# Top-k attention with two MLPs: scores of a head by full-array products, key halves stacked on 128 partitions, and the halves of two weights made by other engines

## The chip, the cores and the metric
One core of one Trainium2 chip runs the whole program in one launch. The metric is the device time of an execution in microseconds; the profile shows one execution of it. PE is TensorE (PEld its weight loads), DVE VectorE, ACT ScalarE, POOL GpSimd, SP the engine that issues the DMAs.

## The reference
Inputs are q, k, v of 4 batches, 8 heads, 576 tokens, 64 elements a head, and five float64 weights. Attention keeps only the 32 largest scores of a row:

```python
scores = scale * np.matmul(q, k.transpose(0, 1, 3, 2))
kth = np.partition(scores, -top_k, axis=-1)[..., -top_k:-top_k + 1]
scores = np.where(scores >= kth, scores, -1000000000.0)
attn = softmax(scores)            # over 576 keys
x = (attn @ v)                    # to 2304 tokens x 512
h = x @ w_in                      # 512 -> 2048
g = np.where(h > 0.0, h, np.exp(np.minimum(h, 0.0)) - 1.0)
x = g @ w_out                     # 2048 -> 512
out = ((x @ w1) * (x @ w2)) @ w3 @ w_out2   # 512 -> 1024 -> 1024 -> 512
```

The choice of the 32 depends on small differences of scores, so the kernel works with high and low halves of its numbers throughout.

## The kernel before
The 2304 tokens are 18 tiles of 128, taken two by two as nine chunks. For each chunk `attention` goes over four head pairs and two tiles, 72 tile-pairs in all; `mlp` then runs the dense layers of the chunk. A tile that spans two batches is scored against both, so there are 80 scored segments for 72 tile-pairs.

Order: each operation is registered with `op(engine, cost, function, reads, writes, rank)`. `Program.emit` then simulates the engines with the written costs, the table `LAT` of handover times, and ranks to which the table `OFF` adds an offset by stage and engine. It writes out one fixed order per engine. An engine's instructions run in that order, so one that waits holds up all behind it on its engine. SP's queue holds all DMAs, loads and transposes alike.

Scores. Queries of a pair and chunk (two heads of 64 rows on 128 partitions, 256 tokens) are loaded into the single buffer `qr`; ACT rounds them to `qh` (L407), POOL makes the rest `ql` (L408). Keys of a batch and pair are loaded once, rounded by ACT (L356) and their rest made by POOL (L357), both into `KT` of 128 partitions by 2 halves by 576, written to DRAM as `KD` and reloaded from there later. For each half of the 576 keys, `qk` (L437) issues six products of 288 columns on half arrays of 64 rows: high with high, high with low, low with high, for two heads each. ACT's L439 then moves the two heads' 288 columns out of `psS`, with the scale. `psS` is one buffer of two banks, so the second half waits for this copy; the columns behind the 288 hold the results of the value product (L491).

Top-k. Per head DVE runs four MAX8 (L447), each but the last followed by a MATCH_REPLACE8 (L449). ACT makes mask and exponential in place (L462, L464), ACT and POOL the two f16 halves (L472, L473), two DMA transposes turn them round, and L491 multiplies by the values.

Weights. Each float64 weight is loaded as words, joined by ACT, DVE and POOL (L542 to L545), normed and converted by `convert`: the high half is a scaled f16 copy; the low half, in the mode used for w_in and w_out, is made on PE as the f32 product with a scaled identity less the high half (L581, L582), and copied out of PSUM (L584). `PAR["hp"]` names the number of sixteenths whose high half POOL makes (L567): all 16 of w_in and all 16 of w_out. w3 and w4 are multiplied with each other first (L686). w1 and w2 are converted with DVE instead (L572).

Dense layers. `unitA` (L747 to L749), `unitO` (L784 to L786) and `unitB` (L826 to L828) issue f16 products of 256 columns, `unitD` (L861 to L863) of 512. Between them ACT, DVE and POOL work on PSUM results; L797 and L846 on DVE are of these, L809 is a small f32 product for a norm.

Of the kernel before, what the change touches and what calls it, by code (L numbers as in the profile page):

```python
# [33 lines left out]
PAR = dict(hp={'wi': 16, 'wo': 16}, whole=(), cd={'wi': [0, 0], 'wo': [0, 0], 'w34': [8, 0], 'w12': [16, 0]}, pv=-577.81, pi=702.591, p34=-453.754, po=123.714, p12=822.408,   # L34
# [5 lines left out]
OFF = {":DVE": 10640, "A0:ACT": 7132, "A0:PE": 7142, "A0:POOL": 10197, "A1:ACT": -310, "A1:PE": -245, "A1:POOL": 1267, "A2:ACT": 133, "A2:PE": -970,  # L40
# [25 lines left out]
       "attsa:ACT": -31679, "attsa:PE": -6029, "attsk:ACT": -21025, "attsk:POOL": 3784, "attsk:SP": 10401, "attsm:ACT": 45222, "attsm:POOL": 39295,  # L66
       "attsp:ACT": -3530, "attsp:POOL": 10399, "attsp:SP": 10858, "attsq:ACT": -8447, "attsq:POOL": 20171, "attsq:SP": 1342, "attss:ACT": 2111,
       "attss:PE": 5478, "attst:DVE": 30531, "attsv:ACT": 22427, "attsv:DVE": 28403, "attsv:SP": 23421, "attsx:ACT": 3955, "attsx:DVE": -7451,
# [3 lines left out]
       "w_in.n:DVE": -17269, "w_in.n:PE": 5551, "w_in:ACT": -10309, "w_in:DVE": -20971, "w_in:POOL": -20121, "w_in:SP": -39372, "w_out.c:ACT": -4070,  # L72
       "w_out.c:PE": -19360, "w_out.c:POOL": -8192, "w_out.n:DVE": -32159, "w_out.n:PE": -3273, "w_out:ACT": -8581, "w_out:DVE": 7470, "w_out:POOL":
       12309, "w_out:SP": -12693, "w_v0:DVE": -38737, "w_v0:PE": 13902, "w_v0:SP": -24224, "w_v1:DVE": -16351, "w_v1:PE": 28175, "w_v1:SP": 59626,
       "w_v:DVE": -23895}
# [120 lines left out]
def kernel(ctx: ExitStack, tc: tile.TileContext, qd, kd, vd, vn, w_in, w_out, w1, w2, w3t, w4, out,  # L196
# [11 lines left out]
    def ring(name, n, shape, dt, space=pool):  # L208
        return [space.tile(shape, dt, name=f"{name}{i}") for i in range(n)]
# [20 lines left out]
    qr = pool.tile([128, 256], F32, name="qr")  # L230
    QH = ring("qh", NQ, [128, 256], F32R)
    QL = ring("ql", NQ, [128, 256], F32R)
# [114 lines left out]
    def att_loads(b, p, pr):  # L347
        ks = nxt("k", NK)
        if ("k", b, p) in seen:
            dma(KT[ks].rearrange("p a s -> p (a s)").bitcast(I32), KD[b, p].bitcast(I32), 128 * S * 8, [("kd", b, p)], [("k", ks)], pr)  # L350
            return ks
        seen.add(("k", b, p))
        rs = nxt("raw", 2)
        kr = raw[rs][:, 0:S]
        dma(kr, kd[b, p], 128 * S * 4, [], [("raw", rs)], pr)
        op("ACT", 574, lambda: A.activation(KT[ks][:, 0], kr, AF.Copy), [("raw", rs)], [("k", ks)], pr)  # L356
        op("POOL", 1240, lambda: G.tensor_tensor(KT[ks][:, 1], kr, KT[ks][:, 0].bitcast(F32), op=OP.subtract),  # L357
           [("raw", rs)], [("k", ks)], pr)
        dma(KD[b, p], KT[ks].rearrange("p a s -> p (a s)").bitcast(F32), 128 * S * 8, [("k", ks)], [("kd", b, p)], pr + PAR["ost"] * STEP)
        return ks  # L360
# [32 lines left out]
    def attention(c, t0, n):  # L393
# [6 lines left out]
        for pair in range(4):  # L400
            base = (t0 * 8 + pair * n * 2 + PAR["a0"] * (c == 0) + PAR["a1"] * (c == 1)) * STEP
            qs = nxt("q", NQ)
            N = n * 128
            pq = base + PAR["oq"] * STEP
            part("q")
            dma(qr[:, 0:N], qd[pair, :, t0 * 128:t0 * 128 + N], 128 * N * 4, [], ["qr"], pq)
            op("ACT", 93 + N * .833, lambda qs=qs: A.activation(QH[qs][:, 0:N], qr[:, 0:N], AF.Copy), ["qr"], [("qh", qs)], pq)  # L407
            op("POOL", 143 + N * 1.904, lambda qs=qs: G.tensor_tensor(QL[qs][:, 0:N], qr[:, 0:N], QH[qs][:, 0:N].bitcast(F32), op=OP.subtract),  # L408
               ["qr", ("qh", qs)], [("ql", qs)], pq)
            for t in range(n):  # L410
                gt = t0 + t
# [578 lines left out]
```

## Time and profile before

| what | value |
|---|---|
| median of 3 runs | 1095.58 us (1093.68 to 1097.67) |
| profiled execution, span of it | 1092.33 us, 1090.5 us |
| busy PE / DVE / ACT / POOL | 998.8 / 870.4 / 806.7 / 694.7 us |
| L437 score products | 960, in groups of six |
| L567 high halves on POOL | 32 |
| L447 MAX8 | 576 |
| first and last first-layer product (L747) | 221.5 and 1023.0 us |

Busy time is the union of an engine's instructions. Matmuls overlap in the pipeline: one of 256 columns is shown with 0.27 us, while the next can start much earlier. So the cost of a group of matmuls is read from starts, not from durations.

### The profile page before, as it was taken

What the parts mean: (1) busy time and instruction counts of PE and PEld (TensorE: products, weight loads), DVE (VectorE), ACT (ScalarE), POOL (GpSimd) and SP (SyncE); (2) the same over time, 40 slices, a digit from 0 to 9 for tenths busy, and PEclk for the clock granted to TensorE, in tenths of its full rate; (3) what the DMA queues carried; (4) which work ended last, traced back from release to release, by engine and by line L of the source; (5) the groups of instructions that cost most, each with busy time, mean ns of one, the idle gap of its engine ahead of it and who ended that gap; (6) DMA issues with size and microseconds to landing.
All of it is one profiled execution on the core that took longest, in us unless ns stands there. A gap on an engine that the chain in (4) does not pass through costs nothing.

```text
span 1090.5 us, 24990 instructions
## 1 busy us (share of the span) xinstructions
PE 998.8 (92%) x9452; PEld 757.9 (69%) x9452; DVE 870.4 (80%) x1936; ACT 806.7 (74%) x1469; POOL 694.7 (64%) x723
## 2 busy tenths in 40 slices
PE   3576789988899999999999999999999999999998
PEld 2323334467788768887886887688768877887875
DVE  4977679999699999989998998978999999742010
ACT  5877587689889967886886778699678868735612
POOL 3999975569838826684784677468447846635711
PEclk9987889999999999999999999999999999999999
DMA  9958799586934766456699436557763563034001
GB/s 317 390 176 237 192 223 268 109 226 203 224 95 143 183 164 155 105 139 134 167 223 240 115 83 169 138 155 190 172 146 87 113 131 69 4 60 88 2 1 39
DMA packets 238681, 165.57 MB, mean 152 GB/s; under 512 B 195808, under 2 KB 208608, under 8 KB 238560
## 3 DMA queue, kind: packets, MB, share of 16 engines
q1 hardware_dynamic: 238560, 163.97, 58.2%
q8 instruction: 74, 1.21, 0.5%
q14 instruction: 47, 0.39, 0.1%
HBM read 95.13 MB, written 21.61 MB: 107 GB/s over the span
## 4 chain that ended last, share of the span: by engine, by line
PE 42%; DVE 17%; DMA 13%; ACT 10%; POOL 10%; issue 6%; SPq 1%; POOLq 0%; DVEq 0%; ACTq 0%
DMA pt<-pi 7%; DVE m L447 7%; DVE wk L449 6%; PE psS L437 4%; PE psR L747 3%; PE psR L749 3%; PE psR L748 3%; PE psY L784 3%; PE psR L826 3%; PE psS L491 3%; PE psY L786 3%; PE psY L785 3%; PE psR L828 3%; PE psR L827 3%; POOL pi L473 2%
## 5 line engine op out<-in xcount | busy, mean ns | idle before, releaser
L447 DVE MAX8 m<-wk 128x8 f32<-128x576 f32 x432 | 310.1, 748 | 0.0
L473 POOL TENSOR_TENSOR pi<-s,pi 128x576 f16<-128x576 f32 x144 | 183.9, 1284 | 105.8 <-ACT pi L472 76.6
L449 DVE MATCH_REPLACE8 wk<-m,wk 128x576 f32<-128x576 f32 x288 | 212.3, 743 | 0.0
L747 PE MATMUL psR<-x,win 128*128 128x256 f16 x576 | 157.2, 273 | 3.1 <-ACT t L768 2.7
L785 PE MATMUL psY<-g,wout 128*128 128x256 f16 x576 | 157.4, 273 | 1.7 <-POOL g L771 1.7
L784 PE MATMUL psY<-g,wout 128*128 128x256 f16 x576 | 157.8, 274 | 0.0
L786 PE MATMUL psY<-g,wout 128*128 128x256 f16 x576 | 157.4, 273 | 0.0
L826 PE MATMUL psR<-x,w 128*128 128x256 f16 x576 | 157.3, 273 | 0.0
L828 PE MATMUL psR<-x,w 128*128 128x256 f16 x576 | 157.0, 273 | 0.0
L749 PE MATMUL psR<-x,win 128*128 128x256 f16 x576 | 157.0, 273 | 0.0
L827 PE MATMUL psR<-x,w 128*128 128x256 f16 x576 | 157.0, 273 | 0.0
L748 PE MATMUL psR<-x,win 128*128 128x256 f16 x576 | 157.0, 273 | 0.0
L439 ACT ACTIVATE s<-psS 128x576 f32<-128x576 f32 (+1 forms) x160 | 103.2, 645 | 60.1 <-POOL pi L473 35.7
L437 PE MATMUL psS<-kt,qh 64*128 64x288 f32 x640 | 90.6, 361 | 32.2 <-ACT s L439 17.7
L447 DVE MAX8 m<-s 128x8 f32<-128x576 f32 x144 | 102.7, 747 | 20.5 <-ACT s L439 20.5
L462 ACT ACTIVATE s<-s,m 128x576 f32<-128x576 f32 x144 | 107.2, 771 | 13.2 <-DVE m L447 12.9
L464 ACT ACTIVATE s<-s,ty 128x576 f32<-128x576 f32 x144 | 106.0, 768 | 6.6 <-POOL ty L458 6.5
L472 ACT ACTIVATE pi<-s 128x576 f16<-128x576 f32 x144 | 95.4, 677 | 19.7 <-DMA pt<-pi 19.5
L437 PEld LDWEIGHTS psS<-kt,qh 64*128 64x128 f32 x640 | 50.9, 196 | 80.3 <-ACT s L439 27.6
L449 DVE MATCH_REPLACE8 wk<-m,s 128x576 f32<-128x576 f32 x144 | 106.2, 744 | 0.0
L769 POOL TENSOR_TENSOR t<-t,t 128x512 f32<-128x512 f32 x72 | 92.2, 1284 | 5.0 <-ACT t L768 3.5
L771 POOL TENSOR_TENSOR g<-t,g 128x512 f16<-128x512 f32 x72 | 83.7, 1164 | 16.1 <-ACT g L770 15.9
(154 smaller groups left out, 2268.6 us busy)
## 6 DMA issues: line engine op xcount, KB each, us to landing
kt<-kd SPq DMA_DIRECT2D x32, 576.0 KB, 4.4
vv<-vd SPq DMA_DIRECT2D x32, 455.0 KB, 4.1
kd<-kt SPq DMA_DIRECT2D x16, 576.0 KB, 4.0
w<-w_in SPq DMA_DIRECT2D x16, 512.0 KB, 6.1
w<-w_out SPq DMA_DIRECT2D x16, 512.0 KB, 8.0
w<-w3t SPq DMA_DIRECT2D x16, 512.0 KB, 5.5
vd<-vv SPq DMA_DIRECT2D x16, 455.0 KB, 4.6
w<-w SPq DMA_DIRECT2D x12, 512.0 KB, 5.0
```

The costliest lines, as they stand in the source:

```text
L447: op("DVE", 665, lambda r=r, src=src, m8=m8, hh=hh: V.max(m8[:, hh, 8 * r:8 * r + 8], src), [skey], [mk], p1 + PAR["ot"] * STEP)
L449: op("DVE", 727, lambda r=r, src=src, w=w, m8=m8, hh=hh: V.match_replace(w, m8[:, hh, 8 * r:8 * r + 8], src, -3.0e38), [skey, mk], [k], p1 ...
L473: op("POOL", 1240, lambda Y=Y, PIs=PIs, hh=hh: G.tensor_tensor(PIs[:, hh, S:2 * S], Y[:, hh], PIs[:, hh, 0:S], op=OP.subtract), hks, [pk], ...
L747: T.matmul(o, lhsT=hi(W)[:, cs], rhs=X[:, 0, kd_, 0:N], start=kd_ == 0, stop=False)
L748: T.matmul(o, lhsT=hi(W)[:, cs], rhs=X[:, 1, kd_, 0:N], start=False, stop=False)
L749: T.matmul(o, lhsT=lo(W)[:, cs], rhs=X[:, 0, kd_, 0:N], start=False, stop=kd_ == 3)
L784: T.matmul(o, lhsT=hi(W)[:, cs], rhs=rh, start=ft == 0 and m % 2 == 0, stop=False, skip_group_check=True)
L785: T.matmul(o, lhsT=hi(W)[:, cs], rhs=rl, start=False, stop=False, skip_group_check=True)
L786: T.matmul(o, lhsT=lo(W)[:, cs], rhs=rh, start=False, stop=ft == 15, skip_group_check=True)
L826: T.matmul(o, lhsT=hi(W)[:, cs], rhs=X[:, 0, kd_, 0:N], start=kd_ == 0, stop=False)
L827: T.matmul(o, lhsT=hi(W)[:, cs], rhs=X[:, 1, kd_, 0:N], start=False, stop=False)
L828: T.matmul(o, lhsT=lo(W)[:, cs], rhs=X[:, 0, kd_, 0:N], start=False, stop=kd_ == 3)
```

## The change
Queries are loaded per tile and pair as two heads side by side, each head's 64 rows twice, on partitions 0 to 63 and 64 to 127. Keys are prepared per head: the 64 rows are loaded twice, ACT rounds all 128 partitions, and POOL replaces partitions 64 to 127 by the rest, so high keys lie over low keys. One product over 128 partitions then holds the high and the low keys for one operand of queries; high and low queries make two products a half of the keys, four a head. The group and its copy out of `psS` are now of one head and all keys. Keys of scores in the dependency table are per head, so a head's top-k depends on its own copy only. The offsets `OFF` and some written costs are other numbers. High halves of w_in and w_out are made by ACT, their low halves leave PSUM by DVE.

```diff
-PAR = dict(hp={'wi': 16, 'wo': 16}, whole=(), ...
+PAR = dict(hv={}, lv={'wi': 16, 'wo': 16}, whole=(), ...
...
-    qr = pool.tile([128, 256], F32, name="qr")
-    QH = ring("qh", NQ, [128, 256], F32R)
-    QL = ring("ql", NQ, [128, 256], F32R)
+    qr = pool.tile([128, 2, 128], F32, name="qr")
+    QH = ring("qh", NQ, [128, 2, 128], F32R)
+    QL = ring("ql", NQ, [128, 2, 128], F32R)
...
-        rs = nxt("raw", 2)
-        kr = raw[rs][:, 0:S]
-        dma(kr, kd[b, p], 128 * S * 4, [], [("raw", rs)], pr)
-        op("ACT", 574, lambda: A.activation(KT[ks][:, 0], kr, AF.Copy), [("raw", rs)], [("k", ks)], pr)
-        op("POOL", 1240, lambda: G.tensor_tensor(KT[ks][:, 1], kr, KT[ks][:, 0].bitcast(F32), op=OP.subtract),
-           [("raw", rs)], [("k", ks)], pr)
+        for hh in range(2):
+            rs = nxt("raw", 2)
+            kr = raw[rs][:, 0:S]
+            dma(kr, kd[b, 2 * p + hh], 128 * S * 4, [], [("raw", rs)], pr)
+            op("ACT", 574, lambda kr=kr, hh=hh: A.activation(KT[ks][:, hh], kr, AF.Copy), [("raw", rs)], [("k", ks)], pr)
+            op("POOL", 1370, lambda kr=kr, hh=hh: G.tensor_tensor(KT[ks][64:128, hh], kr[64:128], KT[ks][64:128, hh].bitcast(F32), op=OP.subtract),
+               [("raw", rs)], [("k", ks)], pr)
...
         for pair in range(4):
-            qs = nxt("q", NQ)
-            N = n * 128
-            pq = base + PAR["oq"] * STEP
-            part("q")
-            dma(qr[:, 0:N], qd[pair, :, t0 * 128:t0 * 128 + N], 128 * N * 4, [], ["qr"], pq)
-            op("ACT", 93 + N * .833, lambda qs=qs: A.activation(QH[qs][:, 0:N], qr[:, 0:N], AF.Copy), ["qr"], [("qh", qs)], pq)
-            op("POOL", 143 + N * 1.904, lambda qs=qs: G.tensor_tensor(QL[qs][:, 0:N], qr[:, 0:N], QH[qs][:, 0:N].bitcast(F32), op=OP.subtract),
-               ["qr", ("qh", qs)], [("ql", qs)], pq)
             for t in range(n):
+                qs = nxt("q", NQ)
+                pq = pr + PAR["oq"] * STEP
+                part("q")
+                dma(qr, qd[2 * pair:2 * pair + 2, :, tok:tok + 128].rearrange("h r t -> r h t"), 128 * 256 * 4, [], ["qr"], pq)
+                op("ACT", 306, lambda qs=qs: A.activation(QH[qs], qr, AF.Copy), ["qr"], [("qh", qs)], pq)
+                op("POOL", 690, lambda qs=qs: G.tensor_tensor(QL[qs], qr, QH[qs].bitcast(F32), op=OP.subtract),
+                   ["qr", ("qh", qs)], [("ql", qs)], pq)
...
-                for half in range(2):
-                    cols = slice(half * 288, half * 288 + 288)
-                    pqk = pr + (PAR["os"] + .25 * half) * STEP
+                for hh in range(2):
+                    pqk = pr + (PAR["os"] + .5 * hh) * STEP
                     for kk, c0, c1 in ks:
-                        def qk(qs=qs, kk=kk, t=t, cols=cols):
-                            for i, (L, e) in enumerate(((QH, 0), (QH, 1), (QL, 0))):
-                                for hh in range(2):
-                                    hs = slice(64 * hh, 64 * hh + 64)
-                                    T.matmul(psS[:, hh, 0:288], lhsT=L[qs][hs, t * 128:t * 128 + 128], rhs=KT[kk][hs, e, cols], start=i == 0, stop=i == 2)
-                        op("PE", 560, qk, [("qh", qs), ("ql", qs), ("k", kk)], ["psS"], pqk)
-                        op("ACT", 540, lambda sS=sS, cols=cols, c0=c0, c1=c1: A.activation(sS[c0:c1, :, cols], psS[c0:c1, :, 0:288], AF.Copy, scale=0.125), ["psS"], [sk], pqk)
+                        def qk(qs=qs, kk=kk, hh=hh):
+                            for half in range(2):
+                                for li, L in enumerate((QH, QL)):
+                                    T.matmul(psS[:, half, 0:288], lhsT=L[qs][:, hh], rhs=KT[kk][:, hh, half * 288:half * 288 + 288], start=li == 0, stop=li == 1)
+                        op("PE", 540, qk, [("qh", qs), ("ql", qs), ("k", kk)], ["psS"], pqk)
+                        op("ACT", 540, lambda ...: A.activation(sS[c0:c1, hh].rearrange("p (a b) -> p a b", a=2), psS[c0:c1, :, 0:288], AF.Copy, scale=0.125), ["psS"], [(*sk, hh)], pqk)
...
-        if spread(i, PAR["hp"].get(nm, 0)):
-            op("POOL", 660, lambda: G.tensor_scalar(hi(W[i]), st, s, None, op0=OP.mult), [*skeys, sk], [(nm, i)], pr)
+        if spread(i, PAR["hv"].get(nm, 0)):
+            op("DVE", 340, lambda: V.tensor_scalar(hi(W[i]), st, s, None, op0=OP.mult), [*skeys, sk], [(nm, i)], pr, lk=True)
         else:
-            op("ACT", 620, lambda: A.activation(hi(W[i]), st, AF.Copy, scale=s), [*skeys, sk], [(nm, i)], pr)
+            op("ACT", 613, lambda: A.activation(hi(W[i]), st, AF.Copy, scale=s), [*skeys, sk], [(nm, i)], pr)
...
-        op("ACT", 480, lambda: A.activation(lo(W[i]), ps, AF.Copy), [pk], [(nm, i, "l")], pr)
+        if spread(i, PAR["lv"].get(nm, 0)):
+            op("DVE", 600, lambda: V.tensor_copy(lo(W[i]), ps), [pk], [(nm, i, "l")], pr)
+        else:
+            op("ACT", 480, lambda: A.activation(lo(W[i]), ps, AF.Copy), [pk], [(nm, i, "l")], pr)
```

## Rows read from the trace of the kernel before

**Rows 1.** The page's busy time, with share of the span and instructions
```profile
PE 998.8 (92%) x9452; PEld 757.9 (69%) x9452; DVE 870.4 (80%) x1936; ACT 806.7 (74%) x1469; POOL 694.7 (64%) x723
```

**Rows 2.** Busy us (instructions) by stage; last three columns PEclk, DMA share, GB/s
```profile
core 0: us, PE busy (x) PEld busy (x) DVE busy (x) ACT busy (x) POOL busy (x), PEclk, DMA share, GB/s
47.00:147.00 100.00, 66.96 (x300) 31.74 (x301) 71.65 (x159) 70.91 (x130) 98.54 (x78) 0.81 0.70 211
147.00:221.00 74.00, 69.63 (x348) 32.58 (x347) 68.97 (x146) 57.73 (x105) 41.51 (x43) 1.00 0.88 207
221.00:327.00 106.00, 93.32 (x1060) 78.46 (x1059) 93.35 (x211) 90.64 (x167) 75.01 (x73) 0.98 0.71 188
327.00:981.00 654.00, 642.11 (x6723) 519.84 (x6722) 593.32 (x1331) 511.57 (x939) 409.05 (x453) 1.00 0.56 137
```

**Rows 3.** Timeline of PE at 884 us: start us, us, instruction
```profile
884.42 0.27 PE L828 MATMUL psR<-x,w 128*128 128x256 f16 x1
...
884.75 0.27 PE L828 MATMUL psR<-x,w 128*128 128x256 f16 x1
884.86 0.39 PE L809 MATMUL psY<-ident,ac 128*128 128x128 f32 x2
885.08 0.27 PE L826 MATMUL psR<-x,w 128*128 128x256 f16 x1
```

**Rows 4.** Timeline of DVE, 943 to 964 us; in brackets idle time before
```profile
943.33 1.42 DVE L447 MAX8 m<-s 128x8 f32<-128x576 f32 x2 [4.32 <-ACT s L439]
...
951.66 1.42 DVE L447 MAX8 m<-wk 128x8 f32<-128x576 f32 x2
962.96 1.41 DVE L797 SCALAR_TENSOR_TENSOR x<-psY,sc,x 128x512 f16<-128x512 f32 x2 [9.89 <-ACT x L796]
```

**Rows 5.** L567 alone by stage: us, POOL busy (instructions), PEclk, DMA share, GB/s
```profile
47.00:147.00 100.00, 50.83 (x32) 0.81 0.70 211
```

**Rows 6.** Timeline of PE around a score group at 502 us
```profile
502.23 0.27 PE L828 MATMUL psR<-x,w 128*128 128x256 f16 x1
502.44 0.54 PE L437 MATMUL psS<-kt,qh 64*128 64x288 f32 x4
502.81 0.29 PE L437 MATMUL psS<-kt,ql 64*128 64x288 f32 x2
503.04 0.39 PE L861 MATMUL psR<-w,pp 128*128 128x512 f16 x1
```

**Rows 7.** The same group, a timeline that ends after its first pair
```profile
502.44 0.40 PE L437 MATMUL psS<-kt,qh 64*128 64x288 f32 x2
```

**Rows 8.** L437 alone by stage: us, PE busy (x), PEld busy (x)
```profile
147.00:981.00 834.00, 96.56 (x870) 62.71 (x870) 1.00 0.61 149
```

**Rows 9.** Groups of instructions: out<-in, count, busy us, mean ns, idle before
```profile
L408 POOL TENSOR_TENSOR ql<-qr,qh 128x256 fp32r<-128x256 f32 x36 | 27.3, 758 | 42.9 <-ACT qh L407 42.2 <-POOL wout L545 0.3 <-ACT ty L502 0.3
L357 POOL TENSOR_TENSOR kt<-raw,kt 128x576 fp32r<-128x576 f32 x16 | 22.6, 1415 | 5.3 <-ACT kt L356 5.3
L407 ACT ACTIVATE qh<-qr 128x256 fp32r<-128x256 f32 x36 | 14.8, 412 | 8.4 <-PE psS L437 5.7 <-DMA qr<-qd 2.6
L569 ACT ACTIVATE w<-w,sc 128x512 f16<-128x512 f32 x21 | 14.5, 713 | 2.1 <-DVE w L572 1.6 <-DVE sc L312 0.4
L797 DVE SCALAR_TENSOR_TENSOR x<-psY,sc,x 128x512 f16<-128x512 f32 x18 | 12.8, 743 | 55.6 <-ACT x L796 55.5
L356 ACT ACTIVATE kt<-raw 128x576 fp32r<-128x576 f32 x16 | 10.9, 681 | 4.1 <-DMA raw<-kd 4.0
L584 ACT ACTIVATE win<-psY 128x512 f16<-128x512 f32 x16 | 9.6, 610 | 2.5 <-PE psY L582 2.5
```

**Rows 10.** L447 alone by stage: us, DVE busy (instructions)
```profile
0.00:221.00 221.00, 70.82 (x100) 0.92 0.82 238
```

**Rows 11.** PE's waits, the longest: us in total, times, longest
```profile
PE psS L437 <- ACT s L439: 17.7, 14, 4.3
```

**Rows 12.** Timeline of PE where the weight product ends and the first layer starts
```profile
220.65 1.02 PE L686 MATMUL psY<-w,pp 128*128 128x512 f32 x2
221.51 0.27 PE L747 MATMUL psR<-x,win 128*128 128x256 f16 x1
```

More of the change, by code (lines that the diff above doesn't have):

```diff
@@ L32 @@
 FLAT = 2.0 ** -100
-PAR = dict(hp={'wi': 16, 'wo': 16}, whole=(), cd={'wi': [0, 0], 'wo': [0, 0], 'w34': [8, 0], 'w12': [16, 0]}, pv=-577.81, pi=702.591, p34=-453.754, po=123.714, p12=822.408,
+PAR = dict(hv={}, lv={'wi': 16, 'wo': 16}, whole=(), cd={'wi': [0, 0], 'wo': [0, 0], 'w34': [8, 0], 'w12': [16, 0]}, pv=-577.81, pi=702.591, p34=-453.754, po=123.714, p12=822.408,
            pis=-107.607, pos=19.797, p12s=-197.302, p34s=838.328, ci=825.351, co=-921.962, cos=928.659, c12=388.003, m34=497.922, c34=2463.442,
@@ L38 @@
            pvb=-3829.627, lag1=-475.176, lagb=401.111)
-OFF = {":DVE": 10640, "A0:ACT": 7132, "A0:PE": 7142, "A0:POOL": 10197, "A1:ACT": -310, "A1:PE": -245, "A1:POOL": 1267, "A2:ACT": 133, "A2:PE": -970,
[25 rows of a table removed]
-       "attsa:ACT": -31679, "attsa:PE": -6029, "attsk:ACT": -21025, "attsk:POOL": 3784, "attsk:SP": 10401, "attsm:ACT": 45222, "attsm:POOL": 39295,
-       "attsp:ACT": -3530, "attsp:POOL": 10399, "attsp:SP": 10858, "attsq:ACT": -8447, "attsq:POOL": 20171, "attsq:SP": 1342, "attss:ACT": 2111,
-       "attss:PE": 5478, "attst:DVE": 30531, "attsv:ACT": 22427, "attsv:DVE": 28403, "attsv:SP": 23421, "attsx:ACT": 3955, "attsx:DVE": -7451,
[3 rows of a table removed]
[L72 to L75, printed above, removed]
+OFF = {":DVE": 12998, "A0:ACT": 1029, "A0:PE": 7709, "A0:POOL": 27517, "A1:ACT": 718, "A1:PE": -1966, "A1:POOL": -5070, "A2:ACT": 9368, "A2:PE":
[25 rows of a table added]
+       -37249, "att8x:SP": 2491, "attsa:ACT": -34761, "attsa:PE": -24674, "attsk:ACT": -25447, "attsk:POOL": -12314, "attsk:SP": 6109, "attsm:ACT":
+       58721, "attsm:POOL": 42862, "attsp:ACT": -13632, "attsp:POOL": 6842, "attsp:SP": 1004, "attsq:ACT": -6686, "attsq:POOL": 29332, "attsq:SP":
+       2937, "attss:ACT": -4807, "attss:PE": 439, "attst:DVE": 42919, "attsv:ACT": 36078, "attsv:DVE": 24193, "attsv:SP": 27657, "attsx:ACT": 19116,
[3 rows of a table added]
+       "w_in.c:PE": 6093, "w_in.n:DVE": -7844, "w_in.n:PE": 4153, "w_in:ACT": 4398, "w_in:DVE": -6625, "w_in:POOL": -6043, "w_in:SP": -40971,
+       "w_out.c:ACT": -366, "w_out.c:DVE": -7456, "w_out.c:PE": -21835, "w_out.n:DVE": -33383, "w_out.n:PE": -12498, "w_out:ACT": -1295, "w_out:DVE":
+       11860, "w_out:POOL": 17259, "w_out:SP": 13558, "w_v0:DVE": -35479, "w_v0:PE": 32785, "w_v0:SP": -8488, "w_v1:DVE": -18213, "w_v1:PE": 29747,
+       "w_v1:SP": 53184, "w_v:DVE": -41841}
 def conv_modes(n, d, g):
@@ L427, in attention @@
                 part("s")
-                for half in range(2):
-                    cols = slice(half * 288, half * 288 + 288)
-                    pqk = pr + (PAR["os"] + .25 * half) * STEP
+                for hh in range(2):
+                    pqk = pr + (PAR["os"] + .5 * hh) * STEP
                     for kk, c0, c1 in ks:
-                        def qk(qs=qs, kk=kk, t=t, cols=cols):
-                            for i, (L, e) in enumerate(((QH, 0), (QH, 1), (QL, 0))):
-                                for hh in range(2):
-                                    hs = slice(64 * hh, 64 * hh + 64)
-                                    T.matmul(psS[:, hh, 0:288], lhsT=L[qs][hs, t * 128:t * 128 + 128], rhs=KT[kk][hs, e, cols], start=i == 0, stop=i == 2)
-                        op("PE", 560, qk, [("qh", qs), ("ql", qs), ("k", kk)], ["psS"], pqk)
-                        op("ACT", 540, lambda sS=sS, cols=cols, c0=c0, c1=c1: A.activation(sS[c0:c1, :, cols], psS[c0:c1, :, 0:288], AF.Copy, scale=0.125), ["psS"], [sk], pqk)
+                        def qk(qs=qs, kk=kk, hh=hh):
[3 more added lines that the diff above has]
+                        op("PE", 540, qk, [("qh", qs), ("ql", qs), ("k", kk)], ["psS"], pqk)
+                        op("ACT", 540, lambda sS=sS, hh=hh, c0=c0, c1=c1: A.activation(sS[c0:c1, hh].rearrange("p (a b) -> p a b", a=2), psS[c0:c1, :, 0:288], AF.Copy, scale=0.125), ["psS"], [(*sk, hh)], pqk)
                 part("t")
@@ L445, in attention @@
                     for r in range(4):
-                        src, skey = (sS[:, hh], sk) if r == 0 else (w, k)
+                        src, skey = (sS[:, hh], (*sk, hh)) if r == 0 else (w, k)
                         op("DVE", 665, lambda r=r, src=src, m8=m8, hh=hh: V.max(m8[:, hh, 8 * r:8 * r + 8], src), [skey], [mk], p1 + PAR["ot"] * STEP)
@@ L462, in attention @@
                     op("ACT", 667, lambda Y=Y, sS=sS, th=th, hh=hh: A.activation(Y[:, hh], sS[:, hh], AF.Prelu, scale=-1.0, bias=th[:, hh:hh + 1], alpha=FLAT),
-                       [sk, mks[hh]], [(*yk, hh)], p3)
+                       [mks[hh]], [(*yk, hh)], p3)
                     op("ACT", 667, lambda Y=Y, tm=tm, hh=hh: A.activation(Y[:, hh], Y[:, hh], AF.Exp, scale=-1.0 / FLAT, bias=tm[:, hh:hh + 1]),
@@ L470, in attention @@
                 for hh in range(2):
-                    pk, hks = ("pi", ps, hh), [(*yk, hh), sk]
+                    pk, hks = ("pi", ps, hh), [(*yk, hh)]
                     op("ACT", 573, lambda Y=Y, PIs=PIs, hh=hh: A.activation(PIs[:, hh, 0:S], Y[:, hh], AF.Copy), hks, [pk], p4 + .5 * hh * STEP)
@@ L491, in av @@
                                 T.matmul(psA[c0:c1, hh, 0:d], lhsT=PT[pt][:, hh, j % 9, c0:c1], rhs=VV[vs][:, j, hh, 0:d], start=j == 0, stop=j == 13, skip_group_check=True)
-                    op("PE", 880, av, [("v", vs), ("vl", vs), ("pt", pt, 0), ("pt", pt, 1)], [pak], p5)
+                    op("PE", 930, av, [("v", vs), ("vl", vs), ("pt", pt, 0), ("pt", pt, 1)], [pak], p5)
                 fs, us = nxt("xf", NX), nxt("xt", 2)
@@ L542, in load64 @@
         op("ACT", 565, lambda: A.activation(lw, low.bitcast(U32), AF.Copy, scale=2.0 ** -29 * (1 - 2.0 ** -9), bias=7.5 * 2.0 ** -9 - 0.5), rk, lk_, pr)
-        op("DVE", 640, lambda: V.scalar_tensor_tensor(low, high, 3, lw, op0=OP.logical_shift_left, op1=OP.bitwise_or), [*rk, *lk_], wk, pr)
-        op("ACT", 530, lambda: A.activation(d.bitcast(F32), high.bitcast(F32), AF.Sign), rk, key, pr)
+        op("DVE", 597, lambda: V.scalar_tensor_tensor(low, high, 3, lw, op0=OP.logical_shift_left, op1=OP.bitwise_or), [*rk, *lk_], wk, pr)
+        op("ACT", 560, lambda: A.activation(d.bitcast(F32), high.bitcast(F32), AF.Sign), rk, key, pr)
         op("POOL", 1255, lambda: G.tensor_tensor(d, d, low, op=OP.add), rk + wk, key, pr)
@@ L950, in layout @@
     import numpy as np
-    qt = q.transpose(1, 3, 0, 2).reshape(4, 128, NT)
-    kt = k.transpose(0, 1, 3, 2).reshape(B, 4, 128, S)
+    qt = q.transpose(1, 3, 0, 2).reshape(H, D, NT)
+    kt = k.transpose(0, 1, 3, 2)
     idx = np.arange(9 * 128) % S
@@ L956, in layout @@
     return {
-        "qd": np.ascontiguousarray(qt),
-        "kd": np.ascontiguousarray(kt),
+        "qd": np.ascontiguousarray(np.concatenate([qt, qt], axis=1)),
+        "kd": np.ascontiguousarray(np.concatenate([kt, kt], axis=2)),
         "vd": np.ascontiguousarray(vr),
```

56 rows, old and new, of the table OFF are left out of this document.

## The prediction
> **What bounds the kernel now.** The page's utilization comes first: PE 92%, DVE 80%, ACT 74%, POOL 64% [rows 1]. A busy PE need not be a full one, so the second look is at stages [rows 2]. From 327 to 981 us PE is busy 642.11 of 654 us. The third look tells whether that is real work: the f16 matmuls of the dense layers follow each other without a hole, three of them from 884.42 to 884.75, 0.11 us each [rows 3]. So PE bounds this stretch, and all holes longer than a pipeline's own add up to about 12 us in it. DVE is busy 593.32 of the 654: 9% are free, and part of its idle time is spent waiting for what PE makes, 4.32 us for scores at 943 and 9.89 us for a layer's output at 963 [rows 4]. From 147 to 327 us PE is busy 69.63 of 74 and 93.32 of 106 us: nearly bound.
>
> Before that the bound is another. Between 47 and 147 us POOL is busy 98.54 of 100 us and PE 66.96, the latter at a granted clock of 0.81 on average (1.00 is 2.4 GHz, the lower level is 1.2) [rows 2]. 50.83 us of POOL are the 32 high halves of L567 [rows 5].
>
> **Scores, the term that carries the forecast.** One group of six 64-row products can be followed at 502 us [rows 6]. The last f16 matmul ahead of it starts at 502.23 and takes 0.11, so PE would be free at 502.34; the group's first start is 502.44, its third pair's 502.81, and the next stranger starts at 503.04. The group costs 503.04 - 502.34 = 0.70 us. In it are 0.10 of nothing ahead; 0.37 from the first start to the last pair's; 0.23 from there to the stranger, where 288 columns at the pace of 256 in 0.109 need only 0.122, so 0.11 of nothing behind. The first pair lasts 0.40 [rows 7] and the last 0.29 [rows 6]: the first weight load lies bare for 0.11. The two steps between the pairs are therefore (0.37 - 0.11)/2 = 0.13 each.
>
> After the change a group is four full-array products of 288 columns. The nearest row for f32 operands on 128 rows between f16 matmuls is L809: 0.11 from the matmul ahead, its two passes of 128 columns in 0.22, and no hole or bare load on either side [rows 3]. So I count four steps and no hole. A step is 0.122 if the columns set it and 0.13 by the pairs, and a load of 0.11 has little room behind 0.122; four of them are 0.49 to 0.55 (0.55 with one part of a load bare). I take 0.53: 0.17 saved a group, bounds 0.15 and 0.21. Farther off lies the case that the holes remain; it is a rival below.
>
> From 147 to 981 us stand 870 of the 960 products [rows 8], 870/6 = 145 groups. The other 90 lie where PE has holes and count nothing. 145 x 0.17 = **-24.7 us** (-22 to -30).
>
> The Trainium skill has a rule against this edit: "TensorEngine Tiling (Array Packing)", When to Use Tiling, recommends twofold row tiling for a contraction of up to 64, and the change gives that up. By the rule alone three shared steps of 0.122 (0.37) become four (0.49), and 145 x 0.12 = 17 us are lost. The trace shows the packed group at 0.70, not at 0.37, so the rule stands as a rival only.
>
> **Weights.** POOL loses 50.83 us. ACT takes 32 high halves at 0.713 (L569, the same shape), 22.8 us, and loses the 32 low ones of L584 at 0.61, 19.5. DVE gets 32 reads of 128x512 out of PSUM: 0.61 each by ACT's row, 0.743 by DVE's own L797, which reads a second operand [rows 9]; 20 to 24 us. All of it falls between 47 and 147 us. POOL drops there to 98.5 - 50.8 + about 7 of new work (below) = 55 of 100, but DVE rises from 71.65 to about 94 and is the next wall; behind it are PE at its lower clock and the DMA engines' share of 0.70 [rows 2]. The stretch gets shorter only as far as top-k work is put off. There is some to put off: 100 MAX8 have run by 221 us [rows 10] where chunk 0, eight tile-pairs of eight, needs 64. The 36 over are 4.5 tile-pairs, and one takes 9.7 us (first MAX8 at 943.33, end at 953.08 [rows 4]), so 44 us are in hand when the first layer begins. The gain is at least 0 (DVE replaces POOL wholly, or loads come no sooner) and at most 25 us (half of POOL's 50.83, the other half lost to that wall). I take **-8**, a third, nearer to nothing because DVE stands at 94.
>
> **Keys and queries.** Keys are prepared per head: 16 more ACT copies at 0.681, 10.9 us, and 16 more subtractions on POOL, of 64 partitions where the row has 128 (1.415): 11 to 23 us. Queries are prepared per tile: 36 more of L407 at 0.412, 14.8, and of L408 at 0.758, 27.3 us [rows 9]. SP issues 16 more loads of 288 KB and 36 of 128 KB, each in the one queue that also carries the transposes for L491. In sum ACT has 807 + 23 - 19 + 11 + 15 = 837 us, POOL 695 - 51 + 23 + 27 = 694. Neither is a bound; from 327 to 981 us ACT has 22% free and POOL 37% [rows 2], and the work hides beside PE there. But it is queued ahead of things that PE waits for: ACT's copy of the scores out of psS, for which L437 already waits 17.7 us in all [rows 11]; POOL's f16 halves; and the low query itself, which the score groups now need twice as often, through one buffer qr. Lower bound nothing; upper bound one L407 of 0.41 bare at each of 72 tile-pairs, 30 us. I take **+5**, near the lower end, since the free shares are wide. Head 0 can now be searched before head 1 is scored; DVE isn't the bound, so that counts nothing, as do the keys read back, whose tile has its old size.
>
> **Sum.** The profiled execution took 1092.33 us, 1.8 of them outside its span of 1090.5. -24.7 - 8 + 5 = -27.7 gives 1064.6. The median of the runs shown, 1095.58, lies 3.2 above that execution, so 1068. Every rank moves with the new offsets; I price that at nothing, with some us either way.
>
> **Rivals**, in terms of the median.
> - *DVE takes over.* It gets some 22 us of work. If half of what PE gives back in the scores turns into waits for top-k, and the start gives nothing, the time is 1095.6 - 12 = 1083. For it: DVE at 593 of 654. Against it: some of its idle time is waiting for PE, which shrinks as PE gets faster.
> - *The start gives its bound.* -24.7 - 25 + 2 makes 1048. For it: POOL is solid for 100 us. Against it: DVE at 94.
> - *Supply eats it.* Low queries and ACT's copies come 0.35 us late at 72 tile-pairs, +25, and the start gives nothing: 1096, no change. For it: one qr buffer. Against it: the free shares of ACT and POOL.
> - *The holes stay* (slower). If the 0.10 ahead and 0.11 behind belong to f32 scores and their waits and not to half-array products, a group is 0.21 + 0.11 of bare load + 0.49 to 0.52 = 0.81 to 0.84, 0.12 dearer; 145 x 0.12 = +17, +5 for supply, nothing at the start: 1118. It decides from where a group takes more than 0.70. For it: nothing in the rows shows an f32 group on 64 rows without holes. Against it: L809, on 128 rows, has none. The skill's rule above is the same loss without the holes' cause. A cousin, f32 columns at the half pace of L686 (two passes of 512 in 0.86 [rows 12]), would be dearer still; against it, two products of 64 rows move 128 rows together at 0.13 a step.
>
> **Chances.** Forecast (1055 to 1078) 0.52, DVE 0.14, whole start 0.14, supply 0.12, holes 0.08. What lies within 0.3% (3.3 us) can't be told from no change here. Faster: 0.52 + 0.14 + 0.14 and 0.04 of supply = 0.84; same 0.04 of supply; slower its last 0.04 and the holes = 0.12. The range takes in the whole start and the DVE case with some us beyond: 1046 to 1090.
>
> **What would show it.** Right: score groups near 0.53 us with no hole to either neighbour; POOL with idle time from 47 to 147 us; the first L747 before 221.51 [rows 12]. Wrong: groups of 0.70 or more; PE holes at L437 that POOL's ql or ACT's s ends in larger sum than before; DVE solid while PE waits for the transposes of L491.

## The result, and the profile after

The changed kernel takes 1078.38 us in the median (1077.04 to 1080.46) where the kernel before takes 1095.57: 17 us less, ratio 0.9844 with a 95% interval of 0.982 to 0.9869. I forecast 1068 and a range of 1046 to 1090. The direction and the range held; of the 28 us forecast, 11 did not come. The profiled execution took 1077.04 us, its span 1075.3.

Lines of code have moved: the score products are L435 now, the value product is L489, the copy of the scores is L437, MAX8 is L445, the first layer starts with L748.

The page's busy time, to be held against [rows 1]:

```profile
PE 983.4 (91%) x9132; PEld 778.6 (72%) x9132; DVE 889.3 (83%) x1968; ACT 830.3 (77%) x1521; POOL 696.6 (65%) x743
```

POOL and ACT came out as summed (694 and 837 forecast). The stages that answer to [rows 2], busy us of PE, PEld, DVE, ACT and POOL, then granted clock, DMA share and GB/s:

```profile
47.00:147.00 100.00, 81.08 (x394) 40.45 (x395) 98.61 (x212) 92.33 (x166) 67.72 (x64) 0.93 0.96 279
147.00:221.00 74.00, 70.26 (x467) 44.07 (x465) 71.54 (x150) 60.45 (x111) 47.56 (x52) 1.00 0.72 188
221.00:327.00 106.00, 93.77 (x987) 81.43 (x986) 101.74 (x230) 96.83 (x181) 81.85 (x81) 0.94 0.78 190
327.00:966.00 639.00, 614.07 (x6311) 517.44 (x6309) 575.54 (x1287) 506.85 (x939) 427.83 (x474) 1.00 0.62 145
```

Three things are to be seen. From 47 to 147 us POOL is no longer solid, DVE is, at 98.61 us. From 221 to 327 us DVE is solid too, at 101.74 of 106, where it had 93.35. And from 327 us on no engine is solid: PE is busy 96.1% where it had 98.2%, though it has less to do.

A score group, the timeline of PE that answers to [rows 6]:

```profile
503.46 0.27 PE L829 MATMUL psR<-x,w 128*128 128x256 f16 x1
503.49 0.38 PE L435 MATMUL psS<-kt,qh 128*128 128x288 f32 x1
503.70 0.29 PE L435 MATMUL psS<-kt,ql 128*128 128x288 f32 x1
503.83 0.29 PE L435 MATMUL psS<-kt,qh 128*128 128x288 f32 x1
503.96 0.29 PE L435 MATMUL psS<-kt,ql 128*128 128x288 f32 x1
504.10 0.28 PE L827 MATMUL psR<-x,w 128*128 128x256 f16 x1
```

The L829 ahead needs 0.11, so the group runs from 503.57 to 504.10: 0.53 us, four steps of 0.13, no hole to either neighbour. The first product's recorded start, 503.49, lies inside the f16 matmul's time; its weight load stands in the trace of PEld from 503.46 on, beside that matmul.

What PE waits for now: first the longest waits that answer to [rows 11], then the group of the value product.

```profile
PE psS L489 <- ACT s L437: 11.8, 12, 2.9
PE psS L435 <- ACT s L437: 11.3, 15, 1.9
PE psS L489 <- DMA pt<-pi: 10.1, 16, 1.3
```

```profile
L489 PE MATMUL psS<-vv,pt 128*128 128x65 f16 (+3 forms) x2240 | 83.5, 194 | 23.5 <-ACT s L437 11.8 <-DMA pt<-pi 10.1 <-DVE xf L506 1.0
```

The same group in the trace of before, a row not shown so far:

```profile
L491 PE MATMUL psS<-vv,pt 128*128 128x65 f16 (+3 forms) x2240 | 83.0, 194 | 11.3 <-DMA pt<-pi 7.2 <-ACT s L439 2.2 <-DVE xf L508 1.6
```

PE's idle time before the value product doubled, 11.3 to 23.5 us. PE reaches it sooner, and finds that ACT still copies scores out of the same two banks, or that the transposed weights have not landed.

Marks for the way through the run are the first products of the first layer: of chunk 0, chunk 1 and chunk 2, then chunk 1 and chunk 2 before.

```profile
185.27 0.27 PE L748 MATMUL psR<-x,win 128*128 128x256 f16 x1
...
303.48 0.28 PE L748 MATMUL psR<-x,win 128*128 128x256 f16 x1
...
415.19 0.27 PE L748 MATMUL psR<-x,win 128*128 128x256 f16 x1
```

```profile
308.12 0.28 PE L747 MATMUL psR<-x,win 128*128 128x256 f16 x1
...
429.62 0.27 PE L747 MATMUL psR<-x,win 128*128 128x256 f16 x1
```

Chunk 0's starts 36 us sooner than the 221.51 of [rows 12], but part of that is only moved: 83 MAX8 stand ahead of it where 100 stood. Chunk 1's, 4.6 us sooner, is not a like mark either, because the order is another. How many products of one of the three lines of `unitB` had run by the marks of chunk 1 and chunk 2 is the number in the first brackets, first for the changed kernel (L827), then before (L826):

```profile
0.00:303.47 303.47, 16.21 (x56) 5.83 (x56) 0.96 0.87 248
0.00:415.18 415.18, 34.91 (x124) 12.53 (x124) 0.96 0.83 228
```

```profile
0.00:308.11 308.11, 2.18 (x8) 0.78 (x8) 0.93 0.81 229
0.00:429.61 429.61, 33.87 (x124) 12.11 (x124) 0.95 0.75 209
```

At chunk 2's mark the products of all four dense units are equal in number, and the changed kernel has two score groups more done (67 for 65). There it is 14.4 us ahead. So of 15.2 us of span 14.4 were won up to chunk 2 and 0.8 after it (1075.3 - 415.2 = 660.1 for 1090.5 - 429.6 = 660.9), although 93 groups of 0.53 were still to come there, for 95 of 0.70. These are single executions, and those of one kernel differ by 3 to 4 us.

### The profile page after: what moved, and what is told of

Read it like the earlier page. It is cut to its first block, busy times and chain, and to the rows that moved or that the text cites. A ratio compares the mean times of both kernels' runs of the same rounds, so it can differ in the third digit from the quotient of the medians.

```text
span 1075.3 us, 24646 instructions
## 1 busy us (share of the span) xinstructions
PE 983.4 (91%) x9132; PEld 778.6 (72%) x9132; DVE 889.3 (83%) x1968; ACT 830.3 (77%) x1521; POOL 696.6 (65%) x743
## 5 line engine op out<-in xcount | busy, mean ns | idle before, releaser
L445 DVE MAX8 m<-wk 128x8 f32<-128x576 f32 x432 | 311.3, 747 | 0.8
L471 POOL TENSOR_TENSOR pi<-s,pi 128x576 f16<-128x576 f32 x144 | 185.2, 1294 | 92.3 <-ACT pi L470 72.1
L447 DVE MATCH_REPLACE8 wk<-m,wk 128x576 f32<-128x576 f32 x288 | 212.4, 742 | 0.0
L748 PE MATMUL psR<-x,win 128*128 128x256 f16 x576 | 157.2, 273 | 1.5 <-ACT t L837 0.8
L827 PE MATMUL psR<-x,w 128*128 128x256 f16 x576 | 158.4, 275 | 0.0
L828 PE MATMUL psR<-x,w 128*128 128x256 f16 x576 | 157.9, 274 | 0.0
L829 PE MATMUL psR<-x,w 128*128 128x256 f16 x576 | 157.8, 274 | 0.0
L435 PE MATMUL psS<-kt,qh 128*128 128x288 f32 x320 | 113.8, 370 | 17.0 <-ACT s L437 11.3
L460 ACT ACTIVATE s<-s,m 128x576 f32<-128x576 f32 x144 | 108.5, 771 | 25.2 <-DVE m L445 25.0
L437 ACT ACTIVATE s<-psS 128x576 f32<-128x576 f32 (+1 forms) x160 | 103.1, 644 | 29.0 <-POOL pi L471 9.6
L445 DVE MAX8 m<-s 128x8 f32<-128x576 f32 x144 | 104.7, 746 | 14.0 <-ACT s L437 14.0
L462 ACT ACTIVATE s<-s,ty 128x576 f32<-128x576 f32 x144 | 106.8, 768 | 6.1 <-POOL ty L456 6.0
L447 DVE MATCH_REPLACE8 wk<-m,s 128x576 f32<-128x576 f32 x144 | 106.3, 742 | 0.0
L489 PE MATMUL psS<-vv,pt 128*128 128x65 f16 (+3 forms) x2240 | 83.5, 194 | 23.5 <-ACT s L437 11.8
L489 PEld LDWEIGHTS <-pt 128*128 128x128 f16 (+1 forms) x2240 | 76.6, 101 | 35.1 <-issue 17.8
```

The lines of the kernel that those rows point to most:

```text
L445: op("DVE", 665, lambda r=r, src=src, m8=m8, hh=hh: V.max(m8[:, hh, 8 * r:8 * r + 8], src), [skey], [mk], p1 + PAR["ot"] * STEP)
L447: op("DVE", 727, lambda r=r, src=src, w=w, m8=m8, hh=hh: V.match_replace(w, m8[:, hh, 8 * r:8 * r + 8], src, -3.0e38), [skey, mk], [k], p1 ...
L471: op("POOL", 1240, lambda Y=Y, PIs=PIs, hh=hh: G.tensor_tensor(PIs[:, hh, S:2 * S], Y[:, hh], PIs[:, hh, 0:S], op=OP.subtract), hks, [pk], ...
L748: T.matmul(o, lhsT=hi(W)[:, cs], rhs=X[:, 0, kd_, 0:N], start=kd_ == 0, stop=False)
L827: T.matmul(o, lhsT=hi(W)[:, cs], rhs=X[:, 0, kd_, 0:N], start=kd_ == 0, stop=False)
L828: T.matmul(o, lhsT=hi(W)[:, cs], rhs=X[:, 1, kd_, 0:N], start=False, stop=False)
```

## Experiments

Theory A was the prediction's: PE's work sets the end, so what a score group saves arrives. Theory B came from the doubled wait: a tile-pair goes in turn through PE, ACT, DVE, ACT, POOL, SP's transposes and PE again, every engine keeps a fixed order, and a faster PE only waits longer at its next stop. Where nothing else is said, an engine's order of instructions is that of the kernel named, to the last one. Times are medians.

**Score groups by full arrays on the kernel before.**

```diff
-                            for i, (L, e) in enumerate(((QH, 0), (QH, 1), (QL, 0))):
-                                for hh in range(2):
-                                    hs = slice(64 * hh, 64 * hh + 64)
-                                    T.matmul(psS[:, hh, 0:288], lhsT=L[qs][hs, ...], rhs=KT[kk][hs, e, cols], ...)
+                            for hh in range(2):
+                                for i, L in enumerate((QH, QL)):
+                                    T.matmul(psS[:, hh, 0:288], lhsT=L[qs][:, ...], rhs=KT[kk][:, hh, cols], ...)
```

> The kernel before, each engine's order kept, where a score group is four products over all 128 rows (two heads mixed, keys high and low in turn: its scores are not those of the reference) in place of six over 64. Data, loads, other engines as before. Theory A (the holes belong to half-array products, PE sets the end, the 20 us of new waits in the changed kernel come from its order and its added work): groups of 0.53 to 0.54 for 0.69, 145 of them bound, 22 to 25 us faster, 1071 to 1074 beside 1095.6; PE's waits at L437 and L491 as before. Theory B (a faster PE simply runs into top-k and transposes): groups as short, but 8 to 12 us faster, 1084 to 1088, with PE's waits grown by 10 us or more. Theory C (holes belong to f32 scores): no faster than before.

1090.67 us beside 1095.68, ratio 0.9947 (0.9925 to 0.997): 5 us. The timeline of PE at the place of [rows 6]:

```profile
502.23 0.27 PE L828 MATMUL psR<-x,w 128*128 128x256 f16 x1
502.26 0.38 PE L436 MATMUL psS<-kt,qh 128*128 128x288 f32 x1
502.47 0.30 PE L436 MATMUL psS<-kt,ql 128*128 128x288 f32 x1
502.61 0.29 PE L436 MATMUL psS<-kt,qh 128*128 128x288 f32 x1
502.74 0.29 PE L436 MATMUL psS<-kt,ql 128*128 128x288 f32 x1
502.87 0.39 PE L861 MATMUL psR<-w,pp 128*128 128x512 f16 x1
```

The group takes 502.87 - 502.34 = 0.53 us for 0.70, with the same data types and the same waits around it. So the holes belonged to the half-array products, and theory C is out. But the L828 ahead stands at 502.23 in both traces: 76 groups, each some 0.17 shorter, have brought the stream forward by nothing at this point (the trace of before is of an execution 3.2 us below its median, this one of one at its median). From chunk 2's mark on, with the same number of dense products and groups done ahead of it, 658.5 us follow (1089.0 - 430.5) for 660.9: 2.4 us for 95 shorter groups.

```profile
430.48 0.27 PE L747 MATMUL psR<-x,win 128*128 128x256 f16 x1
```

The group of the value product says where it went:

```profile
L491 PE MATMUL psS<-vv,pt 128*128 128x65 f16 (+3 forms) x2240 | 83.7, 194 | 22.1 <-DMA pt<-pi 14.8 <-ACT s L439 4.1 <-DVE xf L508 1.9
```

22.1 us of idle time for 11.3, with nothing else changed. Theory A is out for the size; B's own number, 8 to 12 us, was too high as well.

**A fifth product in each group of the changed kernel**, the same question from the other side.

```diff
-                                for li, L in enumerate((QH, QL)):
-                                    T.matmul(..., start=li == 0, stop=li == 1)
+                                for li, L in enumerate((QH, QL) if half else (QH, QL, QL)):
+                                    T.matmul(..., start=li == 0, stop=li == 2 - half)
```

> The changed kernel, order kept, where each score group has a fifth product (the low queries once more on the first half of the keys, so the scores are slightly others): 0.13 us more of PE in each of 160 groups, 145 of them after 147 us, 19 us. If PE's work sets the end (my prediction): 15 to 19 us slower than the changed kernel, 1093 to 1097. If the end is set by the turn of a tile-pair through all engines (theory B, as the 5 us of 22 in the run with full-array products on the old order say): 3 to 8 us slower, 1081 to 1086, with PE's waits at the value product smaller.

1084.12 us, 5.7 slower than the changed kernel for 19 us more of PE, as B expected. L489's idle time fell from 23.5 to 17.3 us. Chunk 2's first product is 4.0 us late and the rest of the run takes 660.4 us (1079.6 - 419.2) for 660.1, with a fifth product in each of 93 groups there.

```profile
419.17 0.27 PE L748 MATMUL psR<-x,win 128*128 128x256 f16 x1
```

So a microsecond of PE, counted by groups, is worth 0.2 to 0.3 us of the end, in either direction, and in these traces less from chunk 2 on: 2.4 us for some 16, 0.3 for some 12. The page's busy time of PE moved less than the count by groups: 13.8 us down in the run above (998.8 to 985.0), 17.0 up in this one (983.4 to 1000.4); by that measure it is 0.3 to 0.4.

**The weights' edit alone on the kernel before** (`hp={}`, `lv={'wi': 16, 'wo': 16}`, the branch with `V.tensor_copy` for L584; offsets of before).

> The kernel before with the edit of the weights alone: high halves of w_in and w_out by ACT, low halves out of PSUM by DVE, offsets of before. Theory A (POOL was the wall of the start, DVE is the next): the first layer starts 8 to 25 us earlier than 221.5, the whole is 5 to 12 us faster, 1084 to 1091, DVE over 95 of the 100 us from 47 to 147. Rival (DVE takes POOL's place wholly): 1095 within 3, the first layer starts near 221.

1104.37 us, 8.7 slower, ratio 1.008 (1.0059 to 1.01): neither theory. Chunk 0's first layer starts at 195 us, 26 sooner, and DVE is at 98.20 of 100, both as A said. Chunk 1's starts at 326, 18 later than before, but with 64 products of each line of `unitB` ahead of it for 8, and three more score groups; PE's busy time from 221 to 327 us is 80.90 for 93.32, with DVE solid. At chunk 2 the two are about even: 433.40 for 429.62, with 128 products for 124 and three more groups done. Of the 11.6 us that the two spans differ by, 7.8 come after that mark. So nothing of chunk 0's gain is left at chunk 2, and most of the loss comes behind it, where the order is not that of before either. The stages from 47 to 147 and from 221 to 327 us:

```profile
47.00:147.00 100.00, 81.07 (x408) 36.64 (x409) 98.20 (x208) 90.13 (x159) 62.32 (x57) 0.95 0.97 274
221.00:327.00 106.00, 80.90 (x858) 65.82 (x856) 100.65 (x228) 87.76 (x160) 68.02 (x68) 0.90 0.51 146
```

**The changed kernel with the weights' halves as before** (high ones by POOL, low ones by ACT; offsets of the changed kernel).

> The changed kernel with the weights' halves as before (high ones on POOL, low ones out of PSUM by ACT), its offsets kept. If the weights' edit gave the 12 us at the start that a count of PE's work shows: 8 to 14 us slower, 1086 to 1092, POOL solid again from 47 to 147 us and the first layer after 210 us. If it only moved the wall from POOL to DVE: within 4 us of 1078.

1106.56 us, 28 slower, more than either side expected. POOL is solid again, and chunk 1's first layer starts at 329.8, 26 us later than in the changed kernel, chunk 2's 40 us later, at 455.31, with the same dense products done:

```profile
47.00:147.00 100.00, 66.46 (x280) 32.70 (x280) 67.29 (x147) 70.66 (x129) 99.34 (x79) 0.85 0.65 195
```

So all of it is lost before chunk 2, and 11 of the 40 us come back after it (the spans differ by 29.2). This run differs from the kernel before by the scores with their supply and by the offsets, and is 22 us later at chunk 1's mark (329.8 for 308.1, with 16 products of each line of `unitB` done for 8, and one score group less). The second halves of keys and queries fall on a POOL that is solid there; how much of the 22 is theirs and how much is the order's, this pair doesn't tell. In both weight runs the order is one that was not found for them.

**The changed kernel with the offsets of before**, other orders of the same instructions.

> The changed kernel with the offsets of the kernel before, so that the planner writes another order of the same instructions. If the gain of 17 us is that of the instructions: 1075 to 1084. If it is largely that of the order found for them (theory B: what PE saves arrives only where the order brings the waits forward): slower than 1090, with PE's waits at L489 and L435 larger and the first layer of chunk 1 later than 303.5.

1089.12 us, between the two expectations: 10.7 us of the 17 go with the order, 6.5 stay.

**Less supply of queries and keys in the changed kernel** (ACT and POOL make 16 columns instead of 128 or 576 after the first use of each buffer).

> The changed kernel, order kept, where after the first uses of each buffer the high and low halves of queries and keys are made for 16 columns only (the rest stays what it was, so the scores are others): about 27 us less of ACT, 70 us less of POOL, all DMAs as they are. If the added supply of queries and keys on ACT and POOL makes the new waits (theory A, first part), 10 to 15 us faster, 1063 to 1068. If not, 0 to 4 us: 1074 to 1078.

1067.40 us, 11 faster. ACT had 22 us less to do and POOL 64. That is all supply, that of before too. The half of the query work and of the key work that the change added is by this some 5 to 6 us, if half the work is worth half the time.

**No query loads after the first two.**

> The changed kernel, order kept, without the query loads after the first two (queries of the first tiles are scored throughout): 70 loads less on SP's queue and no wait of it for the buffer qr; ACT and POOL make their halves as ever. If the one queue and the one buffer hold up the transposes that the value product waits for: 5 to 10 us faster, 1068 to 1073, with fewer waits of L489 for pt. If ACT's and POOL's work was what the run with little supply saved: within 3 us of 1078.

1080.16 us, but from 1073.43 to 1084.48: no gain that can be told. The loads and their place in SP's queue are not what the run above saved.

**The same cut on each engine in turn**, changed kernel. For DVE, MAX8 rounds 2 and 3 look at `src[:, 0:288]`; for ACT, L460 and L462 work on `Y[:, hh, 0:288]`; for POOL, L471 makes 288 columns of the low half.

> The changed kernel, order kept, where rounds 2 and 3 of top-k look at half the columns (288 of 576; another choice of keys than the reference's): 288 MAX8 shorter by about 0.3 us, 86 us less of DVE. If top-k's pace sets the new waits of PE (theory B), they go: 15 us or more faster, 1060 to 1064. If they come from ACT's and SP's queues or the order (theory A), 6 us or less: 1072 to 1078, mostly in the start where DVE is solid.

> The changed kernel, order kept, where mask and exponential (288 instructions of ACT) work on half the columns, so the weights of the other half are raw scores: about 0.24 us less each, 70 to 86 us less of ACT. The same amount taken from DVE gave 4.7 us. If ACT's queue, behind which the copy of the scores stands, sets the pace from chunk 1 on: 15 us or more faster, 1060 to 1064, and L489's and L435's waits for ACT gone. If no single engine does (theory B): 4 to 8 us, 1070 to 1075.

> The changed kernel, order kept, where POOL makes half the columns of the low halves of the attention weights (144 instructions, about 0.55 us less each, 80 us; the other half stays from the first tiles). If POOL stands in the way of the transposes: 10 us or more faster, 1062 to 1068, and fewer waits of L489 for pt. If no single engine does: 4 to 8 us, 1070 to 1075.

> The changed kernel, order kept, with all three at once: less work on DVE (rounds 2 and 3 of top-k on half the columns), ACT (mask and exponential) and POOL (low halves), 80 us or so on each. If the pace is the turn of a tile-pair through all engines (theory B): the gains add up, 15 to 25 us, 1053 to 1063, until PE alone is the bound; then PE's waits after 327 us are under 12 us. If order alone holds PE back: under 10 us, 1068 or more.

| run | busy time taken away (page) | median us | against 1078.38 |
|---|---|---|---|
| DVE | 889.3 to 816.7, 73 us | 1073.68 | -4.7 |
| ACT | 830.3 to 770.8, 60 us | 1070.81 | -7.6 |
| POOL | 696.6 to 617.0, 80 us | 1068.99 | -9.4 |
| all three | 82, 62 and 80 us | 1056.28 | -22.1 |

The three single gains add up to 21.7 us, and all together gave 22.1. Beside the kernel before, measured along with each (1095.68 for the first row, 1094.19 for the others), the ratios are 0.9795, 0.9786, 0.977 and 0.9656 for the changed kernel's 0.9844; by these the gains are 5.4, 6.4, 8.1 and 20.6 us, which add up as well. From chunk 1's first layer to the end, a like mark since the order is the same, the traces give DVE 1.5 us, ACT 5.7, POOL 8.9 and all three 17.7. So no single one of these engines is the bound from chunk 1 on, POOL (65% busy) counts at least as much as DVE (83%), and each gain leaves the others whole. Engines that bound one after another, each for a stretch, would add up too; that is not ruled out. For POOL such a stretch doesn't show at the scale of chunks: its cut gains 0.4 to 1.8 us in each of the seven steps from chunk 1's mark to chunk 8's.

PE's waits after 327 us, expected under 12 us with all three, stayed above that: PE is idle for 14.2 of the 639 us, where the changed kernel has 24.9, and 11.5 us are waits at the value product, where it has 15.4. In the whole run PE's idle time before the value product is 19.1 us for 23.5:

```profile
327.00:966.00 639.00, 624.77 (x6460) 528.02 (x6458) 512.06 (x1278) 465.43 (x950) 371.53 (x480) 1.00 0.65 147
```

```profile
L489 PE MATMUL psS<-vv,pt 128*128 128x65 f16 (+3 forms) x2240 | 82.7, 195 | 19.1 <-DMA pt<-pi 10.0 <-ACT s L437 8.4 <-DVE xf L506 0.4
```

**A version meant to be faster**: 8 of the 32 high halves by POOL, 8 of the 32 low ones by ACT.

> A version meant to be faster than both, complete: the changed kernel where 8 of the 32 high halves are made by POOL, which has 32 us free between 47 and 147 us, and 8 of the 32 low halves leave PSUM by ACT, so DVE, solid there, has 5 us less and ACT no more than now. If DVE's solid stretch is what the start is worth: 3 to 6 us faster than the changed kernel, 1072 to 1076. The planner's order changes with it, and by the run with the old offsets that alone can cost 10 us: then 1080 to 1090.

1085.66 us, 7.3 slower than the changed kernel, as the warning had it: DVE got 1 us less between 47 and 147 (97.58), POOL 12.6 more (80.27), and the order is another; what the loss is due to, this run doesn't tell. No complete version faster than the changed kernel was found.

## Why the prediction was right in direction and too large

*What bounds the kernel.* The step that failed is the first: "So PE bounds this stretch". PE was busy 642 of 654 us at full pace, and that was true; what followed from it was not. In a ring of engines with fixed orders a 98% busy PE can be one of several that just keep up. 5.0 us for some 24 taken away [rows 8], and 5.7 for 19 added, are the price. The miss lies where I called PE the bound. By my terms some 14 of the 28 us belonged before chunk 2 (8 for the weights, 8.5 for 50 of the 145 groups, less a share of the supply) and some 13 behind it. 14.4 came before chunk 2, 0.8 behind it. The sign was in [rows 4]: DVE waiting 4 to 10 us for what PE makes and ACT passes on, while at other places PE waits for ACT and the transposes. Each engine holding up the others now and then is the picture of a ring, not of one bound. I read it as slack of DVE.

*Scores.* The group was forecast at 0.53 us and takes 0.53; L809 in [rows 3] was the right row for a full-array f32 product among f16 ones. The term -24.7 us was right as a count of PE's work by groups and mis-sized as time: with the order kept it is worth -5. The Trainium skill's rule of twofold row tiling for a contraction of 64 ("TensorEngine Tiling (Array Packing)", When to Use Tiling) would have kept the packed products; here they cost 0.70 and the unpacked 0.53. The same page's Key Properties say that a change of tiling mode drains the engine; the trace agrees as far as it goes: both holes of 0.10 and 0.11 us went when only the row count and the number of products changed.

*Weights.* POOL was the wall and DVE the next one, 98.61 for the 94 forecast, and the low halves took 0.67 to 0.68 us each on DVE (bounds 0.61 and 0.743). That the start came out at the sum I had is luck in part, since its parts don't hold by themselves: the weights' edit alone, on the kernel before, is about even at chunk 2 and slower at the end, and the changed kernel without it is 40 us late there. By these two runs the edit hangs together with the new scores, their supply and the order, which a sum of separate terms can't say.

*Keys and queries.* +5 for the whole run agrees with the half of 11 us that all supply costs. The 7 us of new POOL work in the start, given without its working, came as 6.5 from 47 to 147 us (queries and keys 11.5 for 5.0); POOL stood at 67.72 for the 55 forecast, because other work ran sooner too. What this supply costs where POOL gets no relief by the weights I did not ask: the run without the relief is 22 us late at chunk 1, part of it perhaps by its order.

*The new order*, priced at nothing with some us either way, goes with 10.7 of the 17 us: offsets and instructions fit each other here. Where the changed instructions stood under other offsets, or others under these, the time was 1086 to 1107.

*Rivals.* "DVE takes over" described the stretch up to 327 us but not the rest: 73 us less of DVE gave 4.7. "The start gives its bound" is not borne out: 36 us at chunk 0 were 14.4 at chunk 2, scores and order included. "Supply eats it" named a part, 5 to 6 us. "The holes stay" is refuted.

*Open.* That a turn through all engines sets the pace is argued from the sums and not shown step by step. Which handover closes the ring, the three score buffers, the one buffer `pi` or the banks that scores and values share, was not tried: a larger ring of any of them is a change of memory layout and order at once.

## What to carry to other kernels

An engine that is 98% busy in a fixed order is not proven to be the bound: shorten its work with all orders kept, and see whether the end moves before you sell its microseconds. Where single cuts on three engines each give a little and add up, no one of them is the bound; a tile's turn through all of them is the likely pace, and handovers and order are the next place to look. A mark in the run is a like one only if the same work stands ahead of it: count that before saying where time was won. Two half-array f32 products side by side can cost more than full-array ones in turn; stacking the high and low halves of an operand over all 128 rows was worth 0.17 us in 0.70 on PE.

## What the runs showed of the hardware that was not expected

A tensor_scalar on POOL of 128x512, f32 to f16 (L567 before), took 1.56 to 1.70 us, the f32 one of L762 0.709; ACT does the former in 0.71 to 0.74. The 64-partition subtraction of the keys took 1.412 us where 128 partitions had taken 1.415 [rows 9]: half the partitions saved nothing. From 47 to 147 us the granted clock was 0.93 of 2.4 GHz on average with PE busy 81 us, for 0.81 with 67 us [rows 2].
